# Top-k attention and mixture of depths: the first batch's k and q rows all asked for at once, into w1's buffer

## The chip, the cores and the metric

The kernel runs on one core of one Trainium2 chip. The metric is the device time of one execution in microseconds (us), as a median over runs. Five engines work side by side and meet through semaphores: PE (TensorE, matmuls and transposes; its weight loads are listed apart as PEld), DVE (VectorE), ACT (ScalarE), POOL (GpSimd) and SP (SyncE, which here does nothing but ask for transfers). ACT and SP can both ask for transfers; the requests of SP go down the queue that the profile calls q1, those of ACT down q10.

## The reference

```python
# attention: B, H, S, D = 8, 8, 576, 64, all float32
scores = q @ k.T / sqrt(D)
kth    = 32nd largest score of each row
attn   = softmax over the scores >= kth, the others masked out
x      = (attn @ v), heads laid side by side: B x S x 512
# mixture of depths, per batch
s      = x @ w_gate                      # one gate score for each token
top    = the 128 tokens with the largest s
out    = x;  out[top] += sigmoid(s[top]) * (relu(x[top] @ w1) @ w2)   # F = 1024
```

w1 (512 x 1024) and w2 (1024 x 512) are needed for the first time when the first batch's 128 tokens have been chosen, far into the second batch's attention.

## The kernel before, in words

**Units.** The attention of a batch is cut into 18 units: four tiles of 128 query rows times four pairs of heads, and one tile of 64 rows with two groups. `units` lists all 8 x 18 = 144 of them, and one loop (line 986) runs `n` from -1 to 143. In step `n` several units are in hand at once, each at another stage: the scores of unit `n+1` are multiplied on PE (`multiply`, line 336) and copied out of PSUM by ACT (`keep`, line 353, tile `sc`); DVE looks for a bound of unit `n`'s 32nd largest score (`find_bound`, line 362: sixteen MAX8 into `cand`, then a few small ones into `best`); ACT and POOL prepare for unit `n-1` a row `y` that leaves out what lies above the bound (`what_is_below`, line 959; ACT's `sides`, POOL's `y`); DVE takes unit `n-2`'s exact 32nd value from it (`kth_of`, line 970, tile `next`); the mask (`less`), the exponential and the product with v follow for units `n-3` and `n-4`.

**k and q.** [...] rows that come from DRAM are transposed on PE into PSUM and copied by ACT into `kT` and `qT`. The class `Rows` (line 200) does this for one batch. A batch has four pairs of heads; for each pair there is one tile of k rows and one of q rows, each fetched by two requests of 128 KB (`fetch`, line 222), in the order k0, q0, k1, q1, k2, q2, k3, q3. Rows 512 to 575 of all heads come in two more tiles, `last0` (k) and `last1` (q). The `rows` tiles rotate through three buffers (pool `ld`, line 77). `turn` (line 256) asks for the next tile as soon as its transposes have been given out, so that from the fourth tile on a request waits until PE has read the buffer that it will overwrite.

**The first batch.** Nothing runs ahead of batch 0. Its pair 0 and the last rows are turned ahead of the loop; pairs 1, 2 and 3 are turned in steps 0, 1 and 2, each right ahead of the unit that needs it (line 993). Here SP asks for k0 and ACT for q0, then SP for `last0` and ACT for `last1`; every later tile is asked for by SP alone. ACT's instructions stand in one fixed order, and its requests stand ahead of the load of its function table and of its first copy into `kT`.

**Later batches.** From step 2 on, the transposes of the next batch are slipped into each step, one half tile at a time (`parts`, line 278), with `rows` from the same three buffers.

**Order.** All engine instructions go through `InOrder` (line 35), so each engine runs them in the order in which the program gives them out. SP's requests also stand in one fixed order: the first batch's rows, v of batch 0 (`load_v`, step 1), `wg`, `w1` and `w2` (`load_weights`, line 156, in step 2), the next batch's rows and v. Eight semaphores are handed round for the landing of transfers; a request that takes one over stands behind the landing of the transfer that had it before.

Of the kernel before, what the change touches and what calls it, by code (L numbers as in the profile page):

```python
# [12 lines left out]
FP32 = mybir.dt.float32  # L13
# [18 lines left out]
J = 4  # L32
# [14 lines left out]
def kernel(  # L47
# [12 lines left out]
    P = nc.NUM_PARTITIONS  # L60
    B, H, S, D = q.shape
    HD = H * D
    F = moe_w1.shape[1]
    NHP = H // 2
# [12 lines left out]
    ldpool = ctx.enter_context(tc.tile_pool(name="ld", bufs=3))  # L77
# [75 lines left out]
    w1 = const.tile([P, NDC, F], FP32, name="w1")  # L153
    w2 = const.tile([P, NFC, HD], FP32, name="w2")

    def load_weights():
        sp.dma_start(
            out=wg, in_=dataclasses.replace(moe_w_gate, ap=[[0, P], [1, HD]])
        )
        sp.dma_start(out=w1, in_=moe_w1.rearrange("(c p) f -> p c f", p=P))  # L160
        sp.dma_start(out=w2, in_=moe_w2.rearrange("(c p) n -> p c n", p=P))

    pe, dve, act, pool, sp = (
        InOrder(tc, e)
        for e in (nc.tensor, nc.vector, nc.scalar, nc.gpsimd, nc.sync)
    )
# [6 lines left out]
    def flush():  # L173
        while late:
            late.pop(0)()
# [15 lines left out]
    def room_for_qkv(b):  # L191

        kT = kqpool.tile([P, NHP, R + S], FP32, name="kT")
        qT = kqpool.tile([P, NHP, S], FP32, name="qT")
        return kT, qT, vbufs[b % 2]

    class Rows:  # L200
# [1 line left out]

        def __init__(self, kb, qb, kT, qT, issue=None):
            self.src, self.kT, self.qT = (kb, qb), kT, qT
            self.last = [
                ldpool.tile([R, H, D], FP32, name=f"last{i}", bufs=1) for i in range(2)
            ]
            self.rows = []  # L210
            if issue:
                self.fetch(sp)
                self.fetch(issue)
            for w, dma in enumerate((sp, issue or sp)):
                dma.dma_start(
                    out=self.last[w],
                    in_=self.src[w][:, JP:S, :].rearrange("h p d -> p h d"),
                )
            while len(self.rows) < (3 if issue else 2):
                self.fetch()  # L220

        def fetch(self, dma=sp):
            i = len(self.rows)
            if i == 2 * NHP:
                return
            rows = ldpool.tile([P, J, 2, D], FP32, name="rows")
            for hh in range(2):
                dma.dma_start(
                    out=rows[:, :, hh, :],
                    in_=self.src[i % 2][2 * (i // 2) + hh, 0:JP, :].rearrange(  # L230
                        "(p j) d -> p j d", j=J
                    ),
                )
            self.rows.append(rows)
# [57 lines left out]
    def turn_pair(rows, hp):  # L292
        tr = ps_tr.tile([P, 2, J, P], FP32, name="ptr")
        for w in range(2):
            rows.turn(2 * hp + w, tr[:, w, :, :])
        for w in range(2):
            rows.keep(2 * hp + w, tr[:, w, :, :])
# [8 lines left out]
    def load_v(vb, vs):  # L306
        vt, vpair = vs
        v_rows = vb[:, JP:S, :].rearrange("h p d -> p h d")
        for hh in range(2):
            sp.dma_start(  # L310
                out=vpair[hh * R : (hh + 1) * R, :, hh, 0:D], in_=v_rows[:, hh::2, :]
            )
        for h in range(H):
            sp.dma_start(
                out=vt[:, h, :, 0:D],
                in_=vb[h, 0:JP, :].rearrange("(p j) d -> p j d", j=J),
            )

    def groups(t):

        return NHP // 2 if t == J else NHP
# [11 lines left out]
    def room_for_scores():  # L333
        return ps_sc.tile([P, 2, 2, 512], FP32, name="ps")
# [118 lines left out]
    def room_to_turn():  # L453
        return ps_tr.tile([P, 2, J, P], FP32, name="ptr"), ps_av.tile(
            [P, 512], FP32, name="av"
        )
# [62 lines left out]
    def normalise(b, t, xs):  # L519
        n = R if t == J else P  # L520
        den = sums[0:n, b * NT + t, :]
        divide(n, xs, of_batch[b][0][0:n, t, :], den)
# [362 lines left out]
    def gates(b, t):  # L885
        dot_tile(t, *of_batch[b])
# [42 lines left out]
    for b in range(B - 1):  # L929
        n = (b + 1) * per_batch + mix_at_of.get(b, mix_at)[6]  # L930
# [1 line left out]
        place_steps[n] = b  # L932
    mixtures = {}
    qkv = {0: room_for_qkv(0)}
    first_rows = Rows(k[0], q[0], *qkv[0][0:2], issue=act)
    turn_pair(first_rows, 0)
    turn_all_last(first_rows)
    loading = iter(())
# [4 lines left out]
    def is_unit(n):  # L943
        return 0 <= n < N

    def weigh(sc, tr, av, less):

        turn(sc, tr, less)
        tr_last = turn_last(sc, av, less)
        pT = ptpool.tile([P, 2, J, P], FP32, name="pT")  # L950
        last = ptpool.tile([P, P], FP32, name="last")

        def exp():
            act.activation(pT, tr, AF.Exp, scale=scale)
            act.activation(last, tr_last, AF.Exp, scale=scale)

        return pT, last, exp
# [18 lines left out]
    def mask_of(n, on=None):  # L976
        b, i = divmod(n, per_batch)
        masks[n] = mask(scs[n], next8s[b][:, i, :, :], on)
        if i == per_batch - 1:
            at = 2 * per_batch * b  # L980
            pool.tensor_copy(
                out=seen[:, 1, at : at + 2 * per_batch].rearrange("p (n i) -> p n i", i=2),
                in_=next8s.pop(b)[:, :, :, 7],
            )

    for n in range(-1, N):
        b, i = divmod(n, per_batch)
        if i == 0 and 0 <= b < B - 1:
            qkv[b + 1] = room_for_qkv(b + 1)
            loading = chain(  # L990
                loading, Rows(k[b + 1], q[b + 1], *qkv[b + 1][0:2]).parts()
            )
        if 0 < n + 1 < NHP:
            turn_pair(first_rows, n + 1)
        if n == 1:
            load_v(v[0], qkv[0][2])
        if n == 2:
            load_weights()


        gating = normalised
        if inverting is not None:
            normalised = inverting[0:2]
            vector_late.insert(0, lambda a=inverting: normalise(*a))
            inverting = None
        else:
            normalised = None
        if gating is not None:
            vector_late.append(lambda a=gating: gates(*a))

        if is_unit(n - 4):
            tr, av = room_to_turn()
            pT, last, exp = weigh(scs.pop(n - 4), tr, av, masks.pop(n - 4))
            exp()
        if is_unit(n - 3):
            mask_of(n - 3)
        flush()
        if is_unit(n + 1):  # L1020
            b, t, g = units[n + 1]
            ps = room_for_scores()
            multiply(t, g, *qkv[b][0:2], ps)
            load = next(loading, None) if n >= 2 else None
            half = ps[:, 0, :, HALF : HALF + P]
            if load:
                load[0](half)
            scs[n + 1] = keep(ps)
            if load:
                load[1](half)  # L1030
        if is_unit(n - 4):
            b4, t4, g4 = units[n - 4]
            values(t4, g4, pT, last, av, qkv[b4][2])
            if n in place_steps:
                values_bank[0] = av
                next(mixtures[place_steps[n]])
            if g4 == 0:
                xs = xpool.tile([P, H, DE], FP32, name="xs")
                if t4 == 0:
                    x = xpool.tile([P, NT, HD], FP32, name="x")  # L1040
                    pg = place_and_gate[b4 % 2]
                    of_batch[b4] = x, pg
            keep_values(t4, g4, av, xs)
            if g4 == groups(t4) - 1:
                inverting = b4, t4, xs
                n4 = R if t4 == J else P
                keep_sums(n4, xs, sums[0:n4, b4 * NT + t4, :])
            while kept:
                kept.pop(0)()


        if is_unit(n):
            bests[n] = find_bound(scs[n])
        flush_vector()
        flush_pool()
        if is_unit(n - 2):
            kth_of(n - 2)


        if is_unit(n - 1):  # L1060
            what_is_below(n - 1)

        if gating is not None:
            b, t = gating
            if t == J:
                store(out[b], of_batch[b][0])
                mixtures[b] = mixture(float(b * S), of_batch[b][1], ranks[:, b, :])
        for b in mix_steps.get(n, ()):
            next(mixtures[b], None)
        b, i = divmod(n, per_batch)  # L1070
        if i == v_at and 0 <= b < B - 1:
            load_v(v[b + 1], qkv[b + 1][2])
# [214 lines left out]
```

## Time and profile before

| | before |
|---|---|
| median of 3 runs | 880.07 us (879.43 to 882.60) |
| profiled execution | 877.8 us span |
| DVE busy | 809.9 us, 92% |
| PE busy | 808.4 us, 92% |
| ACT busy | 761.2 us, 87% |
| POOL busy | 709.4 us, 81% |
| rows of q, request to landing | 5.2 us for those of ACT's queue, 2.9 us for SP's (medians) |
| w1 and w2, 2 MB each, request to landing | 10.7 us (median) |

In the profile, "x<-y" names the tile written and the tiles read. Nearly all instructions go through one helper, so they all stand at line 43 and are told apart by their tiles. "SPq" and "ACTq" are requests for transfers, with the time that the engine spent on handing them out; the landing comes later. "idle before <-releaser" is how long an engine had nothing to do ahead of an instruction, and what ended that. PEclk is the granted TensorE clock. The shares above are averages over the whole span, while the change acts on its first twentieth, so the prediction reads that stretch on its own.

### The profile page before, as it was taken

The numbers are of one execution on the slowest core, as the hardware profiler recorded it, in microseconds if no ns is written. First come the engines' busy times: TensorE is split into PE (matmuls) and PEld (weight loads), VectorE is DVE, ScalarE is ACT, GpSimd is POOL, SyncE is SP. The second block draws the span as 40 slices with busy tenths as digits, with TensorE's granted clock in tenths as the row PEclk, the third lists the DMA queues.
The fourth block names the chain that finished last, engine by engine and source line by source line (L and its number), as shares of the span: only waits on it lengthen the run. The fifth ranks groups of instructions, "written<-read, shape, count | busy, mean of one in ns | idle before, by whom it ended". The sixth has DMA issues, their size and how long they took to land. (4 is left out here: it accounts for less than half of the span.)

```text
span 877.8 us, 28118 instructions
## 1 busy us (share of the span) xinstructions
PE 808.4 (92%) x9879; PEld 620.2 (71%) x9879; DVE 809.9 (92%) x4918; ACT 761.2 (87%) x1705; POOL 709.4 (81%) x657
## 2 busy tenths in 40 slices
PE   4599998988999999999999999999999999988875
PEld 3376666666787777877787777877787777767743
DVE  3599999999999999999999999999999999999750
ACT  3599999988999999998999999999999999878710
POOL 2389999888888899888988899888988889879610
PEclk9599999999999999999999999999999999999988
DMA  5681111511132121511242112411323002101021
GB/s 118 146 229 27 38 26 56 105 38 38 62 78 47 38 48 58 105 38 35 77 65 60 38 38 68 105 33 31 87 39 82 18 15 68 15 14 14 12 69 15
DMA packets 122196, 50.36 MB, mean 57 GB/s; under 512 B 116416, under 2 KB 116416, under 8 KB 121024
## 3 DMA queue, kind: packets, MB, share of 16 engines
q1 hardware_dynamic: 118672, 43.91, 20.9%
q0 software_dynamic: 1792, 4.20, 2.8%
q8 instruction: 79, 1.29, 0.6%
q14 instruction: 69, 0.57, 0.2%
q10 hardware_dynamic: 1584, 0.39, 0.2%
HBM read 36.93 MB, written 11.55 MB: 55 GB/s over the span
## 5 line engine op out<-in xcount | busy, mean ns | idle before, releaser
L43 POOL TENSOR_TENSOR y<-sc,sides 128x576 f32<-128x576 f32 x288 | 370.4, 1324 | 105.1 <-ACT sides L43 102.1
L43 DVE MAX8 cand<-sc 128x8 f32<-128x72 f32 x2304 | 330.4, 218 | 21.8 <-ACT sc L43 21.8
L43 POOL TENSOR_SCALAR less<-sc,next 128x576 bf16<-128x576 f32 x141 | 248.6, 1763 | 17.2 <-DVE next L43 14.9
L43 ACT ACTIVATE sides<-sc,seen 128x576 bf16<-128x576 f32 x288 | 221.0, 768 | 4.9
L43 PE MATMUL ptr<-out_of_reach,less 128*128 128x128 bf16 x1136 | 205.1, 220 | 21.6 <-POOL less L43 20.8
L43 PE MATMUL ptr<-ident,sc 128*128 128x128 f32 x1136 | 215.7, 279 | 0.0
L43 DVE MAX8 next<-y 128x8 f32<-128x584 f32 x288 | 204.5, 751 | 2.4 <-POOL y L43 2.2
L43 PE MATMUL ps<-kT,qT 64*128 64x288 f32 (+1 forms) x1280 | 183.6, 435 | 5.4 <-ACT qT L43 3.5
L43 PEld LDWEIGHTS ptr<-ident,sc 128*128 128x128 f32 x1136 | 160.6, 141 | 22.4 <-PE av L43 10.4
L43 PE MATMUL av<-v,pT 128*64 128x65 f32 x4544 | 163.8, 224 | 11.3 <-ACT last L43 9.4
L43 PEld LDWEIGHTS av<-v,pT 128*64 128x64 f32 x4544 | 144.2, 137 | 40.7 <-ACT last L43 29.8
L43 ACT COPY sc<-ps 128x1152 f32<-128x1152 f32 x144 | 160.7, 1116 | 10.1 <-PE ps L43 9.8
L43 PEld LDWEIGHTS <-less 128*128 128x128 bf16 x1296 | 132.7, 103 | 43.9 <-POOL less L43 26.8
L43 ACT ACTIVATE pT<-ptr 128x1024 f32<-128x1024 f32 x142 | 144.0, 1014 | 18.3 <-PE ptr L43 16.0
L43 DVE MAX8 best<-cand 128x8 f32<-128x24 f32 (+2 forms) x864 | 141.9, 200 | 0.0
L43 PEld LDWEIGHTS ps<-kT,qT 64*128 64x128 f32 (+1 forms) x1280 | 99.4, 179 | 44.9 <-issue 21.9
L43 ACT ACTIVATE less<-sc,next 128x576 bf16<-128x576 f32 x143 | 110.7, 774 | 22.9 <-DVE next L43 22.8
L43 DVE MATCH_REPLACE8 cand<-best,cand 128x24 f32<-128x24 f32 (+1 forms) x576 | 102.0, 185 | 0.0
L43 PE MATMUL av<-vpair,last 128*128 128x130 f32 (+1 forms) x314 | 68.1, 317 | 0.0
L43 PE MATMUL y_ps<-w,hT 128*128 128x512 f32 x128 | 63.4, 596 | 0.0
L43 PE MATMUL h_ps<-xeT,w 128*128 128x128 f32 x448 | 59.3, 278 | 0.0
L43 PEld LDWEIGHTS h_ps<-xeT,w 128*128 128x128 f32 x448 | 53.9, 192 | 2.1 <-issue 1.1
(102 smaller groups left out, 868.6 us busy)
## 6 DMA issues: line engine op xcount, KB each, us to landing
rows<-in_k_dram SPq DMA_DIRECT2D x64, 128.0 KB, 3.1
v<-in_v_dram SPq DMA_DIRECT2D x64, 128.0 KB, 3.4
out_dram<-x SPq DMA_DIRECT2D x8, 1024.0 KB, 4.0
rows<-in_q_dram SPq DMA_DIRECT2D x62, 128.0 KB, 2.9
w<-in_moe_w_dram SPq DMA_DIRECT2D x2, 2048.0 KB, 10.7
gate_row<-row_dram SPq DMA_DIRECT2D x7, 288.0 KB, 3.7
last<-in_k_dram SPq DMA_DIRECT2D x8, 128.0 KB, 3.4
vpair<-in_v_dram SPq DMA_DIRECT2D x16, 64.0 KB, 4.6
```

The source lines that it names most:

```text
L43: return lambda *a, **kw: self._tc.keep_in_program_order(fn(*a, **kw))
```

## The change

All eight row tiles of batch 0 get a home of their own: 16 KB of each partition, which is the room of `w1`, is cut into eight pieces of 2 KB, and the tiles of batch 0 are put there in place of the three rotating buffers. With a home for each tile no request has to wait for PE to free a buffer, so all eight are asked for ahead of the loop, the k tiles by SP and the q tiles by ACT. `w1` may not be overwritten before the fourth pair has been turned, so `load_weights` moves from step 2 to step 4. The aim is that the data of pairs 1 to 3 is there when PE comes to them. Batch 1 and later batches use the rotating buffers as before, which batch 0 no longer touches.

```diff
-        def __init__(self, kb, qb, kT, qT, issue=None):
-            self.src, self.kT, self.qT = (kb, qb), kT, qT
+        def __init__(self, kb, qb, kT, qT, issue=None, homes=None):
+            self.src, self.kT, self.qT, self.homes = (kb, qb), kT, qT, homes
...
-            while len(self.rows) < (3 if issue else 2):
-                self.fetch()
+            while len(self.rows) < (2 * NHP if homes else 2):
+                self.fetch(issue if homes and len(self.rows) % 2 else sp)
...
-            rows = ldpool.tile([P, J, 2, D], FP32, name="rows")
+            if self.homes:
+                rows = self.homes[i]
+            else:
+                rows = ldpool.tile([P, J, 2, D], FP32, name="rows")
...
-    first_rows = Rows(k[0], q[0], *qkv[0][0:2], issue=act)
+    homes = w1.rearrange("p c (u m) -> p (c u) m", m=J * 2 * D)
+    homes = [
+        homes[:, i, :].rearrange("p (j h d) -> p j h d", j=J, h=2) for i in range(2 * NHP)
+    ]
+    first_rows = Rows(k[0], q[0], *qkv[0][0:2], issue=act, homes=homes)
...
-        if n == 2:
+        if n == NHP:
             load_weights()
```

In the built program ACT gives out six more requests (q1, q2 and q3, two each) between its request for `last1` and the load of its function table, and SP six for k1, k2 and k3 behind `last0`. Of the six on ACT's queue, the first waits for nothing; the second takes over the semaphore of q0's first request, the third that of q0's second, the fourth that of `last1`, the fifth and sixth those of q1's two requests. SP's stand in the same way behind k0, `last0` and k1. The first batch-1 rows now stand ahead of v of batch 0 on SP, without a wait for PE; the request for `w1` waits for PE's last read of its room. The order of the computing instructions on PE, DVE, ACT and POOL is the same as before.

## Prediction

> **What bounds the kernel now.** I read the page's slices first, then the busy time of three stretches, then the waits of the first 60 us, and last the order of time of PE, SP and ACT there.
>
> The slices (22 us each) and the three stretches:
>
> ```profile
> DVE  3599999999999999999999999999999999999750
> PEclk9599999999999999999999999999999999999988
> ```
>
> ```profile
> 0.00:44.03 44.03, 23.45 (x97) 15.92 (x97) 19.88 (x131) 17.89 (x34) 13.28 (x27) 0.77 0.59 133
> 44.03:810.00 765.97, 734.93 (x9310) 567.36 (x9311) 758.79 (x4660) 719.98 (x1618) 673.73 (x611) 1.00 0.24 55
> 810.00:877.80 67.80, 49.98 (x475) 36.88 (x473) 31.23 (x130) 23.34 (x57) 22.41 (x21) 0.91 0.13 31
> ```
>
> The columns are length, then busy PE, PEld, DVE, ACT, POOL, then granted clock, DMA share, GB/s. From 44.03 to 810 us DVE is busy for 758.8 of 766.0 us (99%): it bounds that stretch, and whatever lets it begin earlier moves the end by as much. Up to 44.03 us it is busy for less than half. That is the filling of the pipeline, which the change acts on. Its waits, to 60 us (engine, tile, what it waited for, total us, times, longest):
>
> ```profile
> DVE cand L43 <- ACT sc L43: 21.8, 4, 10.1
> ACT kT L43 <- PE ptr L43: 13.4, 4, 5.1
> PE ptr L43 <- DMA rows<-in_q_dram: 7.3, 2, 3.8
> PE ptr L43 <- POOL vpair L147: 7.1, 1, 7.1
> ```
>
> DVE waits for scores, these for kT, that for transposes, and those twice for q rows: 3.8 us in pair 2, 3.4 us in pair 3. (The last line names POOL, but the first transposes need k0 too, whose second half landed at 7.0 us by the trace.) PE in order of time:
>
> ```profile
> 12.81 1.97 PE L43 MATMUL ptr<-ident,rows 128*128 128x128 f32 x8
> 15.95 2.29 PE L43 MATMUL ps<-kT,qT 64*128 64x288 f32 x8 [1.18 <-ACT qT L43]
> 18.17 1.12 PE L43 MATMUL ptr<-ident,rows 128*128 128x128 f32 x4
> 23.10 1.05 PE L43 MATMUL ptr<-ident,rows 128*128 128x128 f32 x4 [3.81 <-DMA rows<-in_q_dram]
> 25.32 2.29 PE L43 MATMUL ps<-kT,qT 64*128 64x288 f32 x8 [1.17 <-ACT qT L43]
> 32.21 1.09 PE L43 MATMUL ptr<-ident,rows 128*128 128x128 f32 x4 [3.44 <-DMA rows<-in_q_dram]
> ```
>
> And the requests that explain both waits, with what ACT does first:
>
> ```profile
> 15.29 5.24 SPq L43 DMA_DIRECT2D rows<-in_q_dram  x4
> 28.80 1.21 SPq L43 DMA_DIRECT2D rows<-in_q_dram  x2
> ```
>
> ```profile
> 2.10 0.65 ACTq L43 DMA_DIRECT2D last<-in_q_dram  x1
> 2.79 1.28 ACT L43 ACT_TABLE_LOAD   x1 [2.79 <-issue]
> 9.12 0.59 ACT L43 COPY kT<-ptr 128x512 f32<-128x512 f32 x1 [5.05 <-PE ptr L43]
> ```
>
> q2 is asked for at 19.3 us and q3 at 28.8 us, as soon as PE has left a buffer, and lands three us later. ACT's table load ends at 4.1 us and then ACT idles for 5 us: it has slack at the start, but only up to 9.12 us.
>
> [...] one request of SP holds it for 6.2 us (38.56 us) while an earlier transfer is out. So ACT's requests that wait hold ACT. [...] with both queues loaded 225 and 237 GB/s moved from 3 to 5 us, and 178 with SP's alone from 10 to 14 us. [...] transposes take 421 ns up to 43 us against 279 over the span; the records of the clock show a release at 19.74 us, which the wait for q2 wastes, half clock from 23.16 us, and release for good at 43.64 us.
>
> **The change part by part.**
>
> (1) *Waits for q2 and q3 removed.* All row transfers are asked for by about 10 us. There are eighteen of 128 KB (16 row requests, two for the last rows), 2.36 MB; at 170 to 237 GB/s that is 10 to 14 us from the first packets at 2.2 us, so everything lands by 12 to 16 us. Pair 2 is wanted at 20 us, pair 3 at 26 us. The two waits go: 3.81 + 3.44 = 7.25 us.
>
> (2) *Requests added on ACT.* Six by 0.65 us (the row of `last`) are 3.9 us, but what counts is the sixth, which stands behind the landing of q1's second half. That is the fifth of its queue; with as many of SP's interleaved, ten transfers (1.31 MB) must land. Up to 7 us before moved 151+225+237+182+171 KB (GB/s times 1 us from 2 us on) = 0.97 MB; the remaining 0.34 MB at 171 to 237 GB/s take 1.5 to 2.0 us, and the trace shows some 0.6 us from the last packet to the landing: 9.1 to 9.6 us, say 9.4. Then request 0.65, table load 1.28: ACT is free at 11.4 us and not at 4.1. Its first copy into kT moves from 9.12 to 11.4 us: +2.3 us. Behind it stand ACT's other copies, the first matmul and the first sc, so all of unit 0 moves by +2.3: sc from 12.91 to 15.2 us. From below: landing at 8.6 us (when k1 landed before) gives +1.5. From above: the q stream at the lower rate with its worst engine late, 11.5 us, +4.4.
>
> (3) *The chain after that.* With the data there, a unit costs turning (1.97), two copies (1.1) and multiplying (2.29): sc to sc 5.38 us, as units 0 to 1 show (12.91 to 18.29). At half clock sc of units 0, 1, 2 start at 15.2, 20.6, 26.0 us. For unit 3, ACT first has the `seen` and `sides` of unit 0 (ends 2.86 us after sc of unit 2 starts, 27.66 to 30.52 before): 28.9 us, no longer q3; from kT's copy to sc it is 3.89 us (33.33 to 37.22): sc of unit 3 at 32.8 us, against 37.22. Gain 4.5 us: 7.25 removed, 2.3 given back, 0.5 taken by `sides`. From there to DVE's continuous work (unit 4's cand, 44.03 us) the distance of 6.8 us is that of DVE, ACT and POOL and stays.
>
> (4) *The clock.* Without the idle stretches, PE works for 4.2 us on end (multiply 2.29, next turn 1.97), then idles 1.2. Before, a window with 2.96 busy of 3.41 us released the clock, one with 2.24 did not. [...] I take release after the second stretch (22.5 us). Then multiplying takes 1.24 us (as at 45.27 us) and not 2.29, for units 2 and 3: 2 x 1.0 = 2.0 us more. Release after the first stretch adds unit 1 and pair 2's turn, some 1.9; none leaves 4.5.
>
> (5) *At no cost.* The weights: w1 waits for PE's last turn of pair 3 (25 to 28 us), so it goes out some 10 us earlier than at 37.5 and not later; its first use is at 229 us. wg is wanted by the first gate, two tiles in, near 60 us. v is asked for by about 17 to 23 us instead of 30 to 37 and first read at about 40 (46.8 before). Batch 1's second k tile still queues behind the weights; its turn is four steps of 5 us after its predecessors' begin. DVE, PE and POOL have the same instructions.
>
> Sum: -7.25 + 2.3 + 0.5 - 2.0 = -6.45, say -6.5 us: 880.07 - 6.5 = 873.6.
>
> **The rivals.** *Nothing from the clock, or ACT held longer:* gain 2 to 4.5 us, about 876.3. For it speaks that a window with 3.28 us busy (9.50 to 12.91) did not release the clock, and the lag of single engines at 5 to 7 us, where the last engine landed k0 2 us after the first. *Clock released in the first stretch, or ACT free early:* gain 8 to 9, about 871.5. The bound is DVE's own work: sixteen plus the small MAX8 3.47 us for each of four units and 1.44 for each of two `next`, 16.8 us; begun at 16.3 that ends at 33.1, a gain of 10.9. *A wait in place of the one removed:* the six requests go out in two rounds of 5 us each plus table load, with transfers slowed by each other, and ACT is held to 20 us. Then sc of unit 0 starts at 23.8 us, 8.6 later than in (3), and 4.5 - 8.6 is 4.1 us lost: 884.2, slower. Against it: the fifth and sixth need only the first ten transfers.
>
> **How the numbers follow.** Forecast 0.48, no clock or longer hold 0.26, early clock 0.20, slower 0.06. The end adds its own spread: the three runs differ by 3.2 us and the clock falls to half there (849 us). Range: gains of 2.3 to 9.6 us, 870.5 to 877.8, which leaves out the slow rival and the rims of the others. The bound for faster is 4.4 us: nearly all of the forecast and the early clock, and the upper rim of the second case: 0.73. Same 0.22. Slower by over 4.4 us, 0.05.
>
> **What would show it.** The waits for rows of q by PE gone after 12 us; ACT's table load at about 10 us and its first kT copy near 11.4; sc of unit 3 between 30.5 and 32.8; the granted clock released near 22 us and kept; DVE continuous from about 37.5. Wrong if the ACT queue is held past 13 us, if DVE shows new gaps after 44 us, or if the tail differs by more than its spread.

## The result, and the profile after

The change takes the median from 879.98 us (878.47 to 882.6) to 875.04 us (872.93 to 876.19): 4.9 us less, a ratio of 0.994 with a 95% interval of 0.9921 to 0.9959. In the profiled executions the span goes from 877.75 to 873.23 us. The prediction was 873.6 us, with a range of 870.5 to 877.8.

The slices (now 21.8 us each), and the stretches cut at the new beginning of DVE's continuous work, unit 4's first `cand` at 38.06 us. Columns as before: length, busy PE, PEld, DVE, ACT, POOL, then granted clock, DMA share, GB/s.

```profile
DVE  2899999999999999999999999999999999999850
PEclk9699999999999999999999999999999999999988
```

```profile
0.00:38.06 38.06, 20.64 (x97) 14.80 (x97) 19.88 (x130) 17.70 (x34) 13.26 (x27) 0.87 1.02 228
38.06:805.00 766.94, 735.75 (x9301) 567.46 (x9302) 758.07 (x4653) 718.76 (x1616) 672.58 (x610) 1.00 0.23 52
```

DVE does the same 19.88 us of work in the first stretch, in 38.06 us and not in 44.03: 5.97 us less waiting. The rest stays at 99%. So the whole gain lies in the filling, but 5.97 is more than came out at the end (4.5 between the two spans). The waits of the first 60 us (engine, tile, what it waited for, total, times, longest) show what went, what came, and the first hint of where the rest was lost:

```profile
DVE cand L43 <- ACT sc L43: 16.7, 5, 12.4
ACT L43 <- DMA w<-in_q_dram: 10.3, 1, 10.3
PE ps L43 <- ACT qT L43: 7.9, 4, 2.9
DVE next L43 <- POOL y L43: 1.6, 3, 0.8
```

No wait of PE for q rows is left (7.3 us before); DVE's wait for scores falls from 21.8 to 16.7 us. In its place ACT does no computing for 10.3 us, which the profile puts down to the landing of q rows; they are counted from the start of the span and hold the requests themselves too (2.8 us before). DVE's wait for `y` grows to 1.6 us. ACT and PE in order of time (start, duration, engine, instruction, idle time before it):

```profile
2.79 7.44 ACTq L43 DMA_DIRECT2D w<-in_q_dram  x6
10.26 1.28 ACT L43 ACT_TABLE_LOAD   x1 [10.26 <-DMA w<-in_q_dram]
11.55 0.59 ACT L43 COPY kT<-ptr 128x512 f32<-128x512 f32 x1
```

```profile
7.09 1.94 PE L43 MATMUL ptr<-ident,w 128*128 128x128 f32 x8 [7.09 <-POOL vpair L147]
18.32 2.29 PE L43 MATMUL ps<-kT,qT 64*128 64x288 f32 x8 [1.17 <-ACT qT L43]
23.32 1.24 PE L43 MATMUL ps<-kT,qT 64*128 64x288 f32 x8 [1.18 <-ACT qT L43]
28.50 2.29 PE L43 MATMUL ps<-kT,qT 64*128 64x288 f32 x8 [2.91 <-ACT qT L43]
39.95 2.29 PE L43 MATMUL ps<-kT,qT 64*128 64x288 f32 x8
```

The six requests hold ACT until 10.23 us; the table load and the first kT copy follow at once, at 11.55 us where it was 9.12. PE's multiply takes 2.29 us for unit 1, then 1.24 for unit 2, then 2.29 again for unit 3 and still for unit 5 (39.95 us). The clock tells why. Its recorded changes lie whole multiples of 3.413 us apart in both traces (before: 1, 6, 236, 2 and 5 times from one to the next; after: 2, 4, 235, 2 and 5 times); a window, here and below, is one such step, counted from them. After the change they stand at 21.65, 28.48 and 42.13 us, and the first of these stretches is two windows:

```profile
21.65:25.06 3.41, 2.23 (x17) 1.52 (x17) 3.25 (x28) 1.66 (x4) 0.00 (x0) 1.00 0.88 205
25.06:28.48 3.42, 0.53 (x5) 0.29 (x3) 3.12 (x26) 3.35 (x8) 1.60 (x2) 1.00 0.57 120
28.48:42.13 13.65, 10.79 (x50) 7.11 (x50) 11.46 (x74) 9.02 (x19) 9.22 (x10) 0.50 1.03 333
```

PE is busy for 0.53 of 3.42 us in the second window, while ACT works on `sc`, `sides` and the copies behind them (3.35 us busy), and from 28.48 to 42.13 us the granted clock is 0.50. DVE starts its continuous work in the middle of that, at 38.06 us, and then has two gaps:

```profile
43.86 2.25 DVE L43 MAX8 cand<-sc 128x8 f32<-128x72 f32 x16 [0.82 <-ACT sc L43]
48.30 1.44 DVE L43 MAX8 next<-y 128x8 f32<-128x584 f32 x2 [0.78 <-POOL y L43]
```

### The profile page after: what moved, and what is told of

The parts are those of the page before. It is cut to its first block, busy times and chain, and to the rows that moved or that the text cites. A ratio compares the mean times of both kernels' runs of the same rounds, so it can differ in the third digit from the quotient of the medians.

```text
span 873.2 us, 28111 instructions
## 1 busy us (share of the span) xinstructions
PE 807.2 (92%) x9879; PEld 619.9 (71%) x9879; DVE 810.0 (93%) x4918; ACT 760.6 (87%) x1705; POOL 708.7 (81%) x657
## 3 DMA queue, kind: packets, MB, share of 16 engines
HBM read 36.93 MB, written 11.55 MB: 56 GB/s over the span
## 5 line engine op out<-in xcount | busy, mean ns | idle before, releaser
L43 DVE MAX8 cand<-sc 128x8 f32<-128x72 f32 x2304 | 330.2, 217 | 16.7 <-ACT sc L43 16.7
L43 PEld LDWEIGHTS ptr<-ident,sc 128*128 128x128 f32 x1136 | 160.8, 142 | 22.5 <-PE av L43 10.4
```

The source lines that it names most:

```text
L43: return lambda *a, **kw: self._tc.keep_in_program_order(fn(*a, **kw))
```

## The experiments

All traces are compared at the same five points. "u4" is the start of the first `cand` of unit 4; "u4 to u6" is the time from there to unit 6's, which is 9.9 us where DVE has no gap; "rest" runs from unit 6's to DVE's last event. The last column is the median with the interval of the ratio to the kernel before where there is one; the runs of before beside e1 to e4 had a median of 881.79 us, beside e5 to e8 880.96, beside e9 and e10 880.44.

| kernel | first kT copy | sc of unit 3 | u4 | u4 to u6 | rest | median, us (ratio) |
|---|---|---|---|---|---|---|
| before | 9.12 | 37.22 | 44.03 | 9.88 | 823.8 | 879.98 |
| after | 11.55 | 31.25 | 38.06 | 11.59 | 823.5 | 875.04 (0.9921 to 0.9959) |
| e1 q by SP | 8.51 | 26.44 | 33.25 | 11.59 | 826.7 | 873.32 (0.9897 to 0.9948) |
| e2 q1 by ACT | 8.91 | 28.52 | 35.34 | 9.88 | 825.8 | 873.07 (0.9896 to 0.9943) |
| e3 table first | 12.51 | 30.37 | 37.19 | 11.58 | 826.6 | 877.22 (one run) |
| e4 weights late | 8.65 | 35.59 | 42.41 | 11.92 | 824.3 | 880.50 (0.9977 to 1.001) |
| e5 before, busy | 7.66 | 34.97 | 41.78 | 12.47 | 824.3 | 879.92 (0.9979 to 1.0003) |
| e6 after, busy | 11.72 | 28.61 | 35.43 | 12.68 | 825.0 | 874.58 (0.9914 to 0.9963) |
| e7 q1 by ACT, busy | 6.86 | 22.43 | 29.23 | 9.89 | 826.5 | 868.97 (0.9857 to 0.9901) |
| e8 after again | 12.48 | 29.82 | 36.64 | 9.87 | 826.3 | 873.40 (0.9908 to 0.9951) |
| e9 after, busier | 12.03 | 27.00 | 33.83 | 9.87 | 823.8 | 868.60 (0.9845 to 0.9878) |
| e10 q1 by ACT, busier | 7.98 | 23.30 | 30.14 | 9.86 | 826.2 | 867.90 (0.9837 to 0.9871) |

The first transposes start between 5.8 and 7.8 us from run to run, as k0 lands, so the first column carries that spread of up to 2 us. The first five columns are of one profiled execution each, the medians of 4 to 12 (e3 apart). The intervals of e1, e2, e6 and e8 overlap that of the change, so their medians alone do not tell them from it; those of e7, e9 and e10 lie clear of it, and overlap each other.

One thing can be read down the table. Where the clock was at half when u4 began (after, e1, e3, e4, e5, e6), u4 to u6 took 11.58 to 12.68 us; where it was up by then (before, e2, e7 to e10), 9.86 to 9.89.

### e1: q asked for by SP

```diff
-                self.fetch(issue if homes and len(self.rows) % 2 else sp)
+                self.fetch()
```

> The changed kernel, but the tiles k1 to q3 are all asked for by SP; ACT asks for q0 and last1 alone, as before the change. Theory A (ACT is held by its own requests, which costs the path 2.4 us): the first kT copy goes back from 11.55 to about 9.1 us, sc of unit 0 to 12.9, unit 4's first cand from 38.06 to about 35.7 us, and the time falls to about 872.6 us. Rival B (the second queue is what brings the rows in time): with one queue q1 or q2 lands late, PE waits over 1 us for rows of q in pair 1 or 2, and the time is 875 us or more.

ACT and PE:

```profile
2.79 1.28 ACT L43 ACT_TABLE_LOAD   x1 [2.79 <-issue]
8.51 0.59 ACT L43 COPY kT<-ptr 128x512 f32<-128x512 f32 x1 [4.43 <-PE ptr L43]
13.95 0.59 ACT L43 COPY kT<-ptr 128x512 f32<-128x512 f32 x1 [0.53 <-PE ptr L43]
17.39 0.59 ACT L43 COPY kT<-ptr 128x512 f32<-128x512 f32 x1
```

ACT is free at 4.07 us and waits for PE again. No wait for q rows shows after 6.53 us, though one queue carries nearly all. From 5 to 12 us the transfers move 201 GB/s, and 204 in the profile after with two queues, so the 178 that the prediction read for SP's queue alone was not its limit. Rival B falls: what brings the rows in time is that they are asked for early, not that two queues ask. u4 is 4.8 us earlier than after the change, 2.4 more than expected, since the clock was released at 13.5 us, and not at 21.65 as in the profile after. The clock was at half again from 23.77 to 37.42 us, and u4 to u6 has the same 1.7 us of gaps as after the change. Yet the median is only 1.7 us lower: in this profile the rest is 3.2 us longer (826.7 and 823.5), which is taken up under e9 and e10.

### e2: only q1 asked for by ACT

```diff
-                self.fetch(issue if homes and len(self.rows) % 2 else sp)
+                self.fetch(issue if homes and len(self.rows) == 3 else sp)
```

> The changed kernel, but ACT asks for q0, last1 and q1 alone, whose requests stand behind no transfer later than q0; q2 and q3 are asked for by SP. Theory A (ACT is held by q2 and q3 requests): ACT's table load begins at about 4.2 us and not at 10.26, the first kT copy is at about 9.1 us, the time about 872.6 us. Rival B (any transfers beside the first ones delay k0 and so the first transposes): the first transposes and the kT copy stay over 1 us later than 9.1, and the time stays near 875 us.

```profile
4.21 1.28 ACT L43 ACT_TABLE_LOAD   x1 [4.21 <-DMA w<-in_q_dram]
8.91 0.59 ACT L43 COPY kT<-ptr 128x512 f32<-128x512 f32 x1 [3.42 <-PE ptr L43]
```

The table load at 4.21 us, the kT copy at 8.91 and u4 at 35.34 us are what theory A said (4.2, 9.1, 35.7): it is the requests for q2 and q3, behind landings, that hold ACT. The median is 0.5 us above the 872.6 expected; the traces, and not the medians, tell e2 from the change.

### e3: the table load ahead of the requests

```diff
+            if homes:
+                early = stats.tile([P, 1], FP32, name="early")
+                act.copy(out=early, in_=ident[:, 0:1])
             while len(self.rows) < (2 * NHP if homes else 2):
```

> The changed kernel with one small ACT copy ahead of the requests for q1 to q3, which brings the function table's load to 2.8 us, ahead of them. Theory A: what holds ACT is landings, and the table load of 1.28 us comes on top; the last request ends about when it did (10.3 us, up to 0.7 later, since q1 goes out 1.5 us later), so the first kT copy is at 10.3 to 11.0 us and not at 11.55, the time 873.8 to 874.5 us. Rival: the load delays q1 by as much as it saves, the kT copy stays at 11.5 us and the time at 875.

```profile
2.79 1.28 ACT L43 ACT_TABLE_LOAD   x1 [2.79 <-issue]
7.13 5.34 ACTq L43 DMA_DIRECT2D w<-in_q_dram  x6
12.51 0.59 ACT L43 COPY kT<-ptr 128x512 f32<-128x512 f32 x1 [8.23 <-DMA w<-in_q_dram]
```

Both numbers were wrong (12.51 us for the kT copy; the time is of one execution and carries little). The copy put ahead changed the order in which the eight semaphores are handed round: SP's k1 now comes first, and ACT's first request for q1 stands behind a landing too, so it goes out at 7.13 us and not at 2.79. The last one ends at 12.47 us. The share of the table load can't be read from this run; but it shows the hold once more: the kT copy follows the last request by 0.04 us with the table long loaded, so landings hold ACT, and the load comes on top only where it stands behind.

### e4: the weights late, and nothing else

```diff
-        if n == 2:
+        if n == NHP:
             load_weights()
```

> The kernel before with one part of the change alone: the weights are asked for in step 4 and not in step 2. Both theories of the start: nothing moves, 880 us within 1. Rival C (the weights' transfers disturb the first steps, and moving them is part of the gain): 1 us or more faster, with fewer or shorter waits of DVE between 38 and 60 us.

The ratio of 0.9993 (0.9977 to 1.001) is no difference. u4 is 1.6 us earlier, but k0 landed earlier in this run and the clock was up for 6.8 us from 13.2 us on; both waits for q rows are there (7.8 us), and u4 to u6 (11.92 and not 9.88) takes it back. Rival C falls.

### e5 and e6: PE kept busy in its waits

```diff
+    def keep_busy(times):
+        spare = ps_av.tile([P, 512], FP32, name="spare", tag="av")
+        for i in range(times):
+            at = i % 4 * P
+            pe.transpose(spare[:, at : at + P], ident, ident)
+
+    keep_busy(22)
     turn_pair(first_rows, 0)
     turn_all_last(first_rows)
+    keep_busy(6)
...
             turn_pair(first_rows, n + 1)
+            keep_busy((4, 4, 14)[n])
```

> The kernel before, with 50 spare transposes of the identity on PE (22 ahead of pair 0, 6 after the last rows, then 4, 4 and 14 after pairs 1, 2 and 3) where PE would wait; their result is not used. They are to keep the granted clock up from about 8 us on. Theory D (half clock in the first 44 us costs more than the waits for q rows): the multiplies of units 0 to 4 take about 1.24 us and not 2.29, each request for q goes out earlier too, unit 4's first cand moves from 44.03 to about 36 us, and the time falls to about 872 us although the waits for q2 and q3 are still there. Rival: the clock falls back in each wait all the same, or the spare transposes push the needed ones; unit 4's cand is within 2 us of 44 and the time at 879 us or more.

> The changed kernel with the same 50 spare transposes. Theory D: the first kT copy stays at 11.5 us (ACT is held by its requests, not by PE), sc of unit 3 moves from 31.25 to about 27.3 us, unit 4's first cand from 38.06 to about 34.3 us, and the 1.6 us which DVE loses at units 4 and 5 while PE is at half clock (0.82 us for sc, 0.78 us for y) are gone: about 869.6 us. Rival E (those 1.6 us come from the transfers of weights and v that run from 25 to 45 us): both waits of DVE are still there at their size.

PE in e5:

```profile
12.85 1.24 PE L43 MATMUL ps<-kT,qT 64*128 64x288 f32 x8 [0.74 <-ACT qT L43]
18.74 1.09 PE L43 MATMUL ptr<-ident,rows 128*128 128x128 f32 x4 [4.07 <-DMA rows<-in_q_dram]
21.00 2.29 PE L43 MATMUL ps<-kT,qT 64*128 64x288 f32 x8 [0.32 <-ACT qT L43]
28.64 1.09 PE L43 MATMUL ptr<-ident,rows 128*128 128x128 f32 x4 [4.06 <-DMA rows<-in_q_dram]
```

The multiply of unit 1 takes 1.24 us, then PE waits 4.07 us for q2 and the clock falls to half at 17.25 us; the multiply of unit 2 takes 2.29 us. The rival is right for the kernel before: with the spare transposes the clock falls in the wait all the same, and the median does not move (u4, 41.78 us, lies 0.2 us outside what the rival gave). In e6 the clock falls in two other waits. ACT is held (7.61 us), PE waits 3.10 us for `qT` and the clock falls at 11.41 us; it is released at 18.24, and falls again at 31.89, at the end of a window in which PE waits 1.76 us for `kT`. So u4 comes 2.6 us earlier than after the change, but u4 to u6 loses 2.8 (of the 3.4 us of DVE's waits between 28 and 60 us, 0.7 lie ahead of u4):

```profile
DVE next L43 <- POOL y L43: 2.3, 2, 1.6
DVE cand L43 <- ACT sc L43: 1.1, 1, 1.1
```

The median of 874.58 us is that of the change. DVE's waits behind u4 are still there, as rival E has it, but the clock did not stay up: theory D is neither refuted nor shown by this run.

### e7 and e8: the clock up at units 4 and 5

e7 is e2 with the spare transposes of e6; e8 is the changed kernel again.

> The kernel of e2 (ACT asks for q0, last1 and q1 alone) with the same 50 spare transposes. Theories A and D together: first kT copy at about 8.3 us, sc of unit 3 at about 24 us, unit 4's first cand at about 30.6 us, about 867 us, the fastest of all; against the kernel before with spare transposes it shows what the early requests bring when the clock is the same, some 5 us. Rival: with the faster PE the rows of pair 1 or 2 are late and PE waits for them, so that it is no faster than 870 us.

> The changed kernel unaltered, beside the other three on the same chip: 875 us within 1, the first kT copy at 11 to 12 us, and[...] unit 4's first cand within 1.5 us of 38.06.

In e7 the clock is up from 4.22 to 24.7 us and again from 28.11 us. First kT copy, sc of unit 3 and u4 (6.86, 22.43, 29.23 us; expected 8.3, 24, 30.6) are early by about the 1.3 us by which the first transposes began early (5.76 us). There is no gap after u4. The median of 868.97 us is 2 us above the 867 expected. e7 is 11 us below e5, where some 5 us were expected; e5 has the same spare transposes and two waits for q rows of 4.07 and 4.06 us, so that with the half clock of 17.25 to 34.3 us they cost more than their own length.

e8 answers rival E. In this run the clock of the unaltered changed kernel, once released at 18.46 us, was at half from 28.7 to 35.5 us only, so up when DVE's continuous work began (36.64 us):

```profile
31.55 2.29 PE L43 MATMUL ps<-kT,qT 64*128 64x288 f32 x8 [1.76 <-ACT kT L43]
37.02 0.23 PE L43 MATMUL ptr<-out_of_reach,less 128*128 128x128 bf16 x1 [1.21 <-POOL less L43]
37.87 1.24 PE L43 MATMUL ps<-kT,qT 64*128 64x288 f32 x8
```

u4 to u6 takes 9.87 us and has no gap, while the transfers go on at the same time (busy PE, PEld, DVE, ACT, POOL, clock, DMA share, GB/s):

```profile
38.00:48.00 10.00, 9.54 (x126) 7.36 (x128) 10.00 (x67) 9.88 (x23) 8.36 (x9) 1.00 0.95 212
```

DVE is busy for 10.00 of 10.00 us with the DMA engines at 0.95; in the profile after, which has the gaps, they were at 0.78 from 38.06 to 48.06 us. With the split of the table, six profiles against six, this says that the 1.6 us are lost to the clock and not to the transfers. The expectation for u4 (38.06 within 1.5) held; the first kT copy (12.48 us, not 11 to 12) and the time (873.4, not 874 to 876) missed by half a microsecond each. The lost 1.6 us are not the whole story, though: unit 6 begins 3.1 us earlier than in the first profile after the change, but this execution took 874.59 us where that one took 874.99, since its rest is 2.8 us longer.

### e9 and e10: the clock up throughout

```diff
-    keep_busy(6)
+    keep_busy(20)
...
-            keep_busy((4, 4, 14)[n])
+            keep_busy((4, 4, 18)[n])
+        if n in (3, 4):
+            keep_busy(10)
```

e9 is e6 with these; e10 is e7 with the last two.

> The kernel of e6 (the changed one with spare transposes) with more of them where its clock fell back: 20 after the last rows, where PE waits for the held ACT, 18 after pair 3, and 10 more at the beginning of steps 3 and 4. ACT's requests are untouched. Theory D (e6 gained nothing because the clock fell back at 11.4 and at 31.9 us): the clock stays up from about 5 us, multiplies take 1.24 us throughout, sc of units 0 and 3 are at about 14 and 26.3 us, unit 4's first cand at about 33 us with no gap of DVE after it, and the time is about 870 us. Rival (the hold of ACT alone decides): unit 4's cand stays near 35 us, the time at 874.

> The kernel of e7 (ACT asks for q0, last1 and q1 alone, with spare transposes) with 18 after pair 3 and 10 at the beginning of steps 3 and 4. In e7 the clock fell back only from 24.7 to 28.1 us and DVE lost nothing by it, so about the same as e7: 868 to 869 us, and against e9 it shows what holding ACT costs with the clock up in both, about 2.4 to 3 us in unit 4's first cand. Rival: the added spare transposes push the needed ones and it is 1 us or more slower than e7.

e9 with ACT held all the same:

```profile
10.73 1.28 ACT L43 ACT_TABLE_LOAD   x1 [10.73 <-DMA w<-in_q_dram]
12.03 0.59 ACT L43 COPY kT<-ptr 128x512 f32<-128x512 f32 x1
27.00 1.12 ACT L43 COPY sc<-ps 128x1152 f32<-128x1152 f32 x1 [1.57 <-PE ps L43]
```

```profile
5.46:60.00 54.54, 45.39 (x489) 35.56 (x487) 43.16 (x293) 43.02 (x91) 31.62 (x34) 1.00 0.81 186
```

The clock is 1.00 from 5.46 us on. u4 is at 33.83 us (about 33 expected), u4 to u6 is without a gap, and the median is 868.60 us (about 870): 6 us less than e6, which differs from it by spare transposes alone; their intervals do not meet. That shows theory D. With the clock up in both, holding ACT costs 3.7 us at u4 (33.83 against 30.14), somewhat more than the 2.4 to 3 expected. In the medians 0.7 us of that shows (868.60 and 867.90), which the intervals do not separate: in the profiles e10 loses 2.4 us in the rest, which e9 does not (826.2 against 823.8).

Half of that goes with the clock again. In e1, e2, e3, e6, e7, e8 and e10 it was at half for one window of 3.41 us between 785 and 800 us, and in all seven DVE waited 1.35 us at one place, the first `next` after the loop; in the other five neither is seen. Ahead of it PE waits some 2.36 us for `less`, in all twelve. How the windows fall on that wait goes with the difference: in the seven, one window held nearly all of it and PE was busy for 1.03 to 1.15 us; in the five, no window there had under 1.72 us. The busiest of the seven (e8) and the least busy of the five (after):

```profile
789.87:793.28 3.41, 1.15 (x11) 0.96 (x13) 3.41 (x25) 1.03 (x3) 3.41 (x3) 1.00 0.02 2
793.06:796.48 3.42, 1.72 (x17) 1.34 (x17) 3.42 (x26) 1.05 (x4) 3.42 (x4) 1.00 0.00 0
```

The two are executions of one kernel: in e8 one window held 2.26 us of PE's wait (789.77 to 792.13 us), in the profile after 1.70 us (792.40 to 794.76). That the window at half clock brings DVE's wait is read from the twelve traces; it was not tried. The remainder, part of it between 250 and 262 us, is open.

e10 has the lowest median, 867.90 us, ratio 0.9854 (0.9837 to 0.9871), but does not stand clear of e9 and e7.

## Why the prediction was right

The time lay in the range and 1.4 us above the forecast: the mechanism of the first three steps was right, and the fourth and what came behind it were so in part. Step by step:

- *(1) The waits for q2 and q3 go.* Right: no wait of PE for rows after 7.09 us. By the trace the last rows landed at 15.9 us (12 to 16 predicted). e1 adds that the second queue was not needed for it.
- *(2) ACT is held.* Right, in cause and size: q1's second half landed at 9.66 us (9.4; that the transfers of both queues move in turn was the author's estimate, and from 3 to 5 us before the change q1 moved 0.24 MB and q10 0.22 MB), the first kT copy came at 11.55 us (11.4), 2.43 us later than before (2.3). e1 and e2 take the hold away and get the copy at 8.5 to 8.9 us.
- *(3) The chain.* sc of unit 3 at 31.25 us, within the 30.5 to 32.8 given.
- *(4) The clock.* Half right. It was released at 21.65 us, near the 22.5 us that the author's estimate had, and unit 2's multiply took 1.24 us. The step also had unit 3 at 1.24 us and the clock kept. It fell at 28.48 us, behind a window in which PE, now early for unit 3, had waited for a `qT` that stands behind ACT's `sides` (2.91 us): 2.29 us for unit 3. The 2.0 us of this term were about 1.5, and all of it from unit 2: 1.05 us of its multiply, and some 0.4 of its turn (1.61 us and not 1.97), which the term had left out. The busy time that it took as enough for a release (2.96 us) is no measure either: a window with 3.28 us did not release the clock in e1 (6.70 to 10.11 us), one with 2.79 did in e7 (0.81 to 4.22). So u4 came at 38.06 us, a gain of 5.97 where the sum said 6.45, and the other terms held.
- *What failed, and met one of the prediction's own signs of being wrong (a new gap of DVE after 44 us, 0.78 us ahead of 48.30): "the distance of 6.8 us is that of DVE, ACT and POOL and stays", after which DVE was to be continuous.* The distance held (31.25 to 38.06), the continuity did not. The forecast counted PE out as soon as DVE had begun; but at half clock until 42.13 us PE was late for unit 5's sc, and by it ACT and POOL for `y`: u4 to u6 took 11.59 us and not 9.88, so 1.7 us were given back. e8 (clock up, no gap) and e9 show that it is the clock. 5.97 - 1.71 leaves 4.26 us in this profile; 0.26 come back in the rest, which makes the 4.52 of the spans.
- *(5) At no cost.* Right: e4 finds nothing in the place of the weights.

Of the rivals, the early clock was seen in e8 (released at 18.46 us) but with a later landing of k0 (first transposes at 7.75 us) and a longer rest, and gave no more; the slower case would have needed ACT to be held to 20 us.

## What to carry to other kernels

The requests that stood behind landings held everything behind them in their engine's stream here: six on each queue, five of them behind landings, took 7.44 us of ACT and 7.73 us of SP after the change. Put requests that may wait on an engine with no other work (e1), or give the busy engine only those that stand behind the first landings (e2, where two held ACT for 1.39 us). When the filling of a pipeline is shortened, ask whether PE stays busy enough in it to keep its clock, which fell here, up to 800 us, behind windows with at most 1.76 us busy: 88 spare transposes in PE's own waits (e9) took 6.4 us off the changed kernel, more than the 4.9 us of the change itself, while 50 (e6), which left two windows too empty, took off nothing that shows. Count a gain at the start only behind the first steps of the bounding engine's continuous work (1.71 of the 5.97 us were given back there after the change, with PE at half clock), and look for later stretches that take back a part of it (1.5 to 3.2 us of the rest in seven of the kernels here).

## What the runs showed of the hardware

- One window of 3.42 us in which PE was busy for 0.53 us was followed by 13.65 us at half clock after the change (28.48 to 42.13 us): the clock was not released behind the next three windows, each with a wait in it (2.71, 2.34 and 2.33 us busy), but behind the fourth, with 3.41 us busy. The same kernel in another execution (e8) spent 6.8 us there, and its u4 to u6 had no gap.
- The prediction had the clock kept once it was released; it fell behind a window with 0.06 us of PE busy before the change (19.74 to 23.16 us) and 0.53 us after it. The twelve traces show 20 falls up to 800 us, behind windows with 0.00 to 1.76 us of PE busy, and every window that kept the clock up had at least 1.72 us. In e6 a fall came behind 1.65 us busy with no single wait over 1.76 us (28.48 to 31.89 us). Past 800 us two falls do not fit (2.55 us in e8, 2.60 in e10).
- Whether more data in flight slows the first transfers can't be told here: the first transposes began at 7.15 us before and 7.09 us after the change, with eight and ten requests given out by then, but at 7.75 us in the second profile of the changed kernel.
- In e10 the 22 spare transposes ahead of pair 0 held up nothing: they ended at 5.79 us, and PE still waited 1.09 us for k0.
